# Loading every wide operand of a two-part sequence kernel by transposing transfers, and reordering all of its operations

## The chip, the cores and the metric

The kernel runs on one core of a Trainium2 chip. A core has five engines with an instruction stream each: TensorE (PE, matrix products; its weight loads are listed as PEld), VectorE (DVE), ScalarE (ACT), GpSimd (POOL) and SyncE (SP). SP computes nothing here: it issues the transfers (DMAs), in the order of its stream, and so its stream is called the SP queue below. PE writes its results to PSUM, which has eight banks; DVE or ACT must copy them to SBUF (an eviction) before a bank can be used again. The metric is the device time of one execution in microseconds (us).

## The reference

All inputs and the output are bf16. There are two independent heads over S = 2048 steps and D = 640 channels, and their results are concatenated on the channel axis to [1, 2048, 1280].

```python
# head A: a diagonal complex state-space model
dt = exp(log_dt); Lam_bar = exp(dt * (Lambda_re + 1j * Lambda_im))
B_bar = ((Lam_bar - 1) / Lam)[:, None] * (B_re + 1j * B_im)
Bu = einsum("bld,pd->blp", x, B_bar)
for t in range(L):
    h = Lam_bar * h + Bu[:, t, :]                 # 2048 steps, 640 complex states
y = 2 * einsum("blp,dp->bld", hseq, C).real + x * Dskip
# head B: a short and a long convolution over time, channel by channel
k_shift = sum(k_pad[:, t:t + S] * shift_k[:, 3 - t] for t in range(4))
kv = k_shift * v
y = irfft(rfft(kv_pad) * rfft(ssm_k_pad))[:S] + kv * ssm_D
out_B = q * y
```

## The kernel before, in words

One SBUF tile (`arena`) holds all data; regions are named by `LAY`. Every operation is added to a `Program` with its reads and writes, and `emit` issues all operations in the order written out by hand in the string `ORDER`: each token is operation number, engine letter (T PE, V DVE, A ACT, G POOL, S SP) and first PSUM bank. Each engine works through its own tokens in order. `emit` asks for a wait wherever an operation's footprint touches that of an earlier one on another engine or of an earlier transfer; and it declares two operations independent only where neither is already known to come before the other. For pairs that it leaves undeclared, the framework adds waits by its own view of the addresses. Besides, transfers share eight completion counters in turn, so that a transfer waits for the one eight transfers earlier.

**Head A** (class `PartA`). Time is split as 16 rows i by 128 columns; the 640 complex states are 10 blocks j of 64 states, each with real and imaginary parts on 128 partitions. `load_x` (L478) and `load_B` (L472) load x and B in natural layout. `turn_x` (L503, evicted at L508) transposes x on PE; `prep_B` (L522, evicted at L528) transposes B and multiplies it by a complex factor `GM` (made at L420) that comes from the parameters, which are loaded at L340, transposed on PE (L348) and worked on by small DVE and ACT operations of `params`. The product with x is `base` (L533), five 128x512 matmuls for each half PSUM group; `up2`, `up1`, `up0` combine rows i pairwise by rotation matrices `RR` (L552); `coarse` scans over the 128 columns; `down` distributes back (L655; where ACT evicts, an identity matmul at L653 adds the old value on PE). `project` (L687, L692) multiplies by C, evicts at L696 and stores. C goes through a DRAM plane (L488) and one transposing transfer (L489).

**Head B** (class `PartB`), in two halves of 320 channels. k, v, q are loaded in blocks of 80 channels with time on partitions (`load_k` L755 and L759, `load_v` L768). `conv` multiplies and adds the four taps and v on DVE over 128x2560 tiles (L795, L800, L801). `s1` (L820, evicted at L825) and `s2` (L838, evicted at L851) are the two steps of a transform, for the filter ("h") and for kv ("k"); in `s1` for "k" the weights are columns 40 elements apart. `product` (L862 to L869) is the complex product on DVE, four chunks in a half; `r2` (L883, L888) and `r1` (L904, L916 with the factor q) are the inverse.

`setup` makes the transform matrices with iota (POOL), integer operations and Sin on ACT. L286 and L289 make the arguments of `W`; L325 scales `G`.

Of the kernel before, what the change touches and what calls it, by code (L numbers as in the profile page):

```python
# [182 lines left out]
for _name, _n in (("A", 10 * 16 * 130), ("BT", 6400), ("RR", 5120), ("W", 4096), ("G", 8192), ("XT", 10240), ("AS", 10240),  # L183
                  ("Y", 10240), ("T", 7680), ("H0", 5120), ("K0", 5504), ("V0", 5120), ("YS", 2560), ("SN", 1024), ("I3", 192), ("E", 64),
                  ("JS", 128), ("F1", 128), ("IDF", 192), ("DG", 640), ("SK", 640), ("DM", 160),
                  ("PV", 70), ("SMALL", 1400)):
    LAY.part(_name, _n)


class Ctx:  # L190
    def __init__(self, nc, tc, arena, psum, ins, out):
# [3 lines left out]
        self.CP = {nc.scalar: nc.scalar.copy, nc.vector: nc.vector.tensor_copy, nc.gpsimd: nc.gpsimd.tensor_copy}  # L195
        self.small_at = LAY.at["SMALL"][0]
# [19 lines left out]
def setup(c):  # L216
# [13 lines left out]
    P.add("js0", {V: .2}, lambda e: e.tensor_scalar_mul(out=JS[:, 0:64], in0=I3[:, 64:128], scalar1=-1.0), outs=[JS[:, 0:64]],  # L230
          ins=[I3[:, 64:128]])
    P.add("js1", {V: .2}, lambda e: e.tensor_copy(out=JS[:, 64:128], in_=I3[:, 128:192]), outs=[JS[:, 64:128]],
# [24 lines left out]
    scr = c.arena[:, LAY.at["A"][0]:LAY.at["A"][0] + 20800]  # L257
    m1 = scr[:, 20000:20064].bitcast(i32)
    q1 = scr[:, 20064:20192].bitcast(i32)
    s1 = scr[:, 20192:20320].bitcast(f32)  # L260
# [12 lines left out]
    offw = f(2)  # L273
    for lo, b, val in ((0, 0, 6144.0), (0, 1, 8192.0), (64, 0, 4096.0), (64, 1, 6144.0)):
        P.add("offw", {V: .1}, lambda e, lo=lo, b=b, val=val: e.memset(offw[lo:lo + 64, b:b + 1], val),
              outs=[offw[lo:lo + 64, b:b + 1]])
    mw = scr[:, 0:4096].bitcast(i32)
    qw = scr[:, 4096:12288].bitcast(i32)
    for ch in range(4):
        mc = mw[:, 512 * ch:512 * ch + 512]  # L280
        qc = qw[:, 1024 * ch:1024 * ch + 1024]
        q4 = qc.rearrange("p (k b c) -> p k b c", k=8, b=2)
        P.add("w_m", {G: .6}, lambda e, mc=mc, ch=ch: e.iota(mc, pattern=[[4, 8], [128, 64]], base=1 + 32 * ch,
                                                               channel_multiplier=0), outs=[mc])
        for b in range(2):
            P.add("w_q", {A: .8}, lambda e, q4=q4, mc=mc, b=b: e.activation(  # L286
                out=q4[:, :, b, :], in_=mc.rearrange("p (k c) -> p k c", k=8), func=FN.Identity, scale=p63, bias=offw[:, b:b + 1]),
                outs=[q4[:, :, b, :]], ins=[mc, p63, offw])
        P.add("w_a", {V: .7}, lambda e, qc=qc: e.tensor_single_scalar(out=qc, in_=qc, scalar=8191, op=ALU.bitwise_and),  # L289
              outs=[qc], ins=[qc])  # L290
        wo = Wt[:, 8 * ch:8 * ch + 8, :].rearrange("p k c -> p (k c)")
        P.add("w_s", {A: 1.15}, lambda e, qc=qc, wo=wo: e.activation(out=wo, in_=qc, func=FN.Sin, bias=npi, scale=SC13),
              outs=[wo], ins=[qc, npi])

    IDF = c.IDF = v("IDF")
    mi = scr[:, 20320:20448].bitcast(i32)
    qi = scr[:, 19000:19384].bitcast(i32)
# [14 lines left out]
    sn = v("SN")  # L312
    for ch in range(4):
# [9 lines left out]
        for el in range(2):  # L323
            go = Gt[:, ri, 32 * bh:32 * bh + 32, el, :]
            P.add("g_k", {V: .47, G: 2.9}, lambda e, go=go, el=el: e.tensor_scalar(  # L325
                out=go, in0=sn.rearrange("p (b a) -> p b a", a=32), scalar1=mk[:, el:el + 1], scalar2=None, op0=ALU.mult),
                outs=[go], ins=[sn, mk])


def params(c):  # L330
# [42 lines left out]
    for lo, mi, val in ((0, 0, 2 ** 30), (0, 1, -2 ** 31), (64, 0, 0), (64, 1, 2 ** 30)):  # L373
# [18 lines left out]
    dc, sg = f(2), f(1)  # L392
    for lo, mi, val in ((0, 0, 1.0), (0, 1, 0.0), (64, 0, 0.0), (64, 1, 1.0)):
        P.add("dc", {V: .1}, lambda e, lo=lo, mi=mi, val=val: e.memset(dc[lo:lo + 64, mi:mi + 1], val), outs=[dc[lo:lo + 64, mi:mi + 1]])
    for lo, val in ((0, 2.0), (64, -2.0)):
        P.add("sg", {V: .1}, lambda e, lo=lo, val=val: e.memset(sg[lo:lo + 64, :], val), outs=[sg[lo:lo + 64, :]])
    na, ma, mb, ga = f(20), f(20), f(20), f(20)
# [7 lines left out]
    P.add("den", {V: .12}, lambda e: e.tensor_scalar(out=den, in0=den, scalar1=sg, scalar2=None, op0=ALU.mult), outs=[den], ins=[den, sg])  # L405
    P.add("na", {V: .13}, lambda e: e.tensor_tensor(out=t3(na), in0=al3[:, 0:10, :], in1=bc(dc.rearrange("p (o m) -> p o m", o=1), [128, 10, 2]),
                                                    op=ALU.subtract), outs=[na], ins=[al3[:, 0:10, :], dc])
    P.add("ma", {V: .13}, lambda e: e.tensor_tensor(out=t3(ma), in0=t3(na), in1=bc(col(lre), [128, 10, 2]), op=ALU.mult), outs=[ma], ins=[na, lre])
    P.add("mb", {V: .13}, lambda e: e.tensor_tensor(out=t3(mb), in0=t3(na), in1=bc(col(lim), [128, 10, 2]), op=ALU.mult), outs=[mb], ins=[na, lim])
    P.add("ga0", {V: .12}, lambda e: e.tensor_tensor(out=t3(ga)[:, :, 0], in0=t3(ma)[:, :, 0], in1=t3(mb)[:, :, 1], op=ALU.subtract),  # L410
          outs=[t3(ga)[:, :, 0]], ins=[t3(ma)[:, :, 0], t3(mb)[:, :, 1]])
    P.add("ga1", {V: .12}, lambda e: e.tensor_tensor(out=t3(ga)[:, :, 1], in0=t3(mb)[:, :, 0], in1=t3(ma)[:, :, 1], op=ALU.add),
          outs=[t3(ga)[:, :, 1]], ins=[t3(mb)[:, :, 0], t3(ma)[:, :, 1]])
    P.add("ga", {V: .13}, lambda e: e.tensor_tensor(out=t3(ga), in0=t3(ga), in1=bc(col(den), [128, 10, 2]), op=ALU.mult), outs=[ga], ins=[ga, den])
    scr = c.arena[:, LAY.at["A"][0]:LAY.at["A"][0] + 20800]
    c.GM = scr[:, 17600:18880]
# [6 lines left out]
    spread("gm", c.GM, ga, {V: 1.55})  # L423
# [7 lines left out]
    s16 = v("K0", 5120, 256).bitcast(i32)  # L431
    phs, phc = v("K0", 0, 2560).bitcast(i32), v("K0", 2560, 2560).bitcast(i32)
# [20 lines left out]
class PartA:  # L453
# [57 lines left out]
    def prep_B(self, u):  # L511
# [15 lines left out]
        def ev(e, B):  # L527
            c.CP[e](out=out, in_=B[:, 0:n])  # L528
# [611 lines left out]
```

## Time and profile before

| | |
|---|---|
| median of 3 runs | 229.06 us (228.41 to 230.14) |
| profiled execution: own time | 229.08 us |
| profiled execution: span, first to last instruction | 227.3 us |
| mean granted TensorE clock | 0.959 |
| busy: PE, DVE, ACT, POOL | 197.0, 181.6, 145.0, 47.4 us |
| moved by the transfers | 24.06 MB, 106 GB/s in the mean |

The profiled execution takes 1.8 us more than its span and is as long as the median run. Busy is time in which an instruction of the engine is under way; matmuls overlap, so the busy time of a group over its count is the time that one costs, and the mean ns of one is its latency. A row gives source line, engine, operation, output and inputs; brackets give the idle time before it and what ended it. SPq and ACTq rows are the issuing of transfers. In the timelines, rows of one kind are merged, with their count.

### The profile page before, as it was taken

To read this page: it belongs to the slowest core of one execution; us is meant where nothing else is said; L and a number is where in the kernel's file an instruction comes from. 1 tells how busy PE (TensorE), PEld (TensorE's weight loads), DVE (VectorE), ACT (ScalarE), POOL (GpSimd) and SP (SyncE) were. 2 spreads that over 40 slices of the span, in tenths; PEclk is the share of its full clock that TensorE was granted. 3 is DMA by queue.
4 is the path that set the end of the run, shared out by engine and by line. 5 is a ranking of instruction groups with operands and counts; after the bars stand their busy time and mean duration, and the time that the engine had idled before them with its cause. 6 is when DMAs were issued, how large, how long until landed. Compare 5 with 4: busy or idle time off the path is not lost.

```text
span 227.3 us, 7898 instructions
## 1 busy us (share of the span) xinstructions
PE 197.0 (87%) x3552; PEld 142.6 (63%) x3566; DVE 181.6 (80%) x217; ACT 145.0 (64%) x173; POOL 47.4 (21%) x45
## 2 busy tenths in 40 slices
PE   0715998999999999999999689997999899997793
PEld 0615544545565687786763566776888787777572
DVE  6797698969999956479999999997962489988730
ACT  2870868849669665579889779757764585148021
POOL 6592091000009400500006900074000000000000
PEclk9975899999999999999999999999979699999998
DMA  5999639999900996394992019031503700016264
GB/s 168 243 219 185 157 63 144 121 151 165 172 1 6 115 138 99 57 217 85 150 143 58 4 33 199 12 89 39 112 32 86 179 3 29 31 38 167 59 147 120
DMA packets 96782, 24.06 MB, mean 106 GB/s; under 512 B 91117, under 2 KB 96749, under 8 KB 96749
## 3 DMA queue, kind: packets, MB, share of 16 engines
q1 hardware_dynamic: 96678, 23.56, 58.7%
q8 instruction: 28, 0.46, 0.9%
q14 instruction: 6, 0.04, 0.1%
q10 hardware_dynamic: 70, 0.01, 0.0%
HBM read 16.68 MB, written 6.88 MB: 104 GB/s over the span
## 4 chain that ended last, share of the span: by engine, by line
PE 61%; DVE 25%; ACT 7%; issue 4%; DMA 1%; ACTq 0%; DVEq 0%
PE acc L687 20%; PE acc L820 10%; PE acc L838 7%; PE acc L533 7%; DVE arena L795 6%; PE acc L883 4%; DVE arena L800 4%; PE acc L692 2%; PE acc L904 2%; PE acc L503 2%; PE acc L522 2%; PE acc L552 1%; PE acc L655 1%; DVE arena L801 1%; DVE arena L420 1%
## 5 line engine op out<-in xcount | busy, mean ns | idle before, releaser
L687 PE MATMUL acc<-arena 128*128 128x320 bf16 x320 | 49.9, 306 | 0.0
L533 PE MATMUL acc<-arena 128*128 128x512 bf16 x188 | 43.9, 381 | 1.7 <-issue 1.3
L825 ACT CAST arena<-acc 128x1024 bf16<-128x1024 f32 x34 | 33.7, 1015 | 11.0 <-PE acc L820 10.9
L687 PEld LDWEIGHTS <-arena 128*128 128x128 bf16 x320 | 29.9, 100 | 12.7 <-issue 1.6
L851 ACT CAST arena<-acc 128x960 bf16<-128x960 f32 (+1 forms) x39 | 34.6, 919 | 4.9 <-PE acc L838 4.3
L696 ACT CAST arena<-acc 128x640 bf16<-128x640 f32 x16 | 11.0, 692 | 33.1 <-PE acc L692 33.1
L533 PEld LDWEIGHTS <-arena 128*128 128x128 bf16 x200 | 18.7, 99 | 20.5 <-issue 0.8
L820 PE MATMUL acc<-arena 64*64 64x64 bf16 x1280 | 28.8, 238 | 1.5 <-DVE arena L673 0.8
L820 PEld LDWEIGHTS <-arena 64*64 64x64 bf16 x1280 | 26.3, 159 | 5.9 <-issue 2.1
L838 PE MATMUL acc<-arena 128*64 128x160 bf16 x512 | 22.5, 244 | 2.1 <-ACT arena L825 1.1
L795 DVE TENSOR_TENSOR arena<-arena 128x2560 bf16<-128x2560 bf16 x15 | 23.7, 1593 | 0.3
L838 PEld LDWEIGHTS <-arena 128*64 128x64 bf16 x512 | 19.2, 115 | 5.0 <-ACT arena L825 1.6
L800 DVE TENSOR_TENSOR arena<-arena 128x2560 bf16<-128x2560 bf16 x12 | 18.8, 1568 | 0.3
L916 DVE TENSOR_TENSOR arena<-acc,arena 128x960 bf16<-128x960 f32 (+1 forms) x12 | 12.1, 1041 | 5.1 <-PE acc L904 5.0
L888 ACT CAST arena<-acc 128x1024 bf16<-128x1024 f32 x13 | 13.1, 1021 | 2.1 <-PE acc L883 1.7
L883 PE MATMUL acc<-arena 64*128 64x128 bf16 x320 | 12.1, 226 | 2.6 <-DVE arena L869 1.7
L671 ACT CAST arena<-acc 128x1024 bf16<-128x1024 f32 (+2 forms) x16 | 13.9, 933 | 0.2 <-PE acc L655 0.2
L825 DVE CAST arena<-acc 128x1024 bf16<-128x1024 f32 x6 | 7.3, 1219 | 8.3 <-ACT arena L825 6.2
L655 PE MATMUL acc<-arena 128*128 128x512 bf16 (+2 forms) x50 | 13.8, 326 | 0.0
L883 PEld LDWEIGHTS <-arena 64*128 64x128 bf16 x320 | 11.0, 145 | 4.5 <-ACT arena L671 2.2
L865 DVE TENSOR_TENSOR arena<-arena 128x1280 bf16<-128x1280 bf16 x16 | 12.8, 822 | 0.8
L862 DVE TENSOR_TENSOR arena<-arena 128x2560 bf16<-128x2560 bf16 x8 | 11.9, 1492 | 1.2 <-ACT arena L851 0.5
(134 smaller groups left out, 287.9 us busy)
## 6 DMA issues: line engine op xcount, KB each, us to landing
out_dram<-arena SPq DMA_DIRECT2D x32, 160.0 KB
arena<-in_A_x_dram SPq DMA_DIRECT2D x16, 160.0 KB
arena<-in_B_ssm_k_dram SPq DMA_DIRECT2D x8, 320.0 KB
arena<-in_B_k_dram SPq DMA_DIRECT2D x8, 320.0 KB
arena<-in_B_v_dram SPq DMA_DIRECT2D x8, 320.0 KB
arena<-in_B_q_dram SPq DMA_DIRECT2D x8, 320.0 KB
arena<-in_A_B_re_dram SPq DMA_DIRECT2D x2, 400.0 KB
arena<-in_A_B_im_dram SPq DMA_DIRECT2D x2, 400.0 KB
```

What stands on the lines that cost most here:

```text
L533: e.matmul(o, lhsT=self.BT[:, j, d, :], rhs=self.XT[:, d, t0:t0 + n], start=(d == 0), stop=(d == 4), skip_group_check=True)
L655: e.matmul(B[:, o:o + 128 * k], lhsT=c.RR[:, n, j, :], rhs=A[:, j, q:q + k, 0:128], start=not by_pe, stop=True, skip_group_check=True)
L671: e.copy(out=o, in_=b)
L687: e.matmul(B[:, 512 * b:512 * b + 320], lhsT=lh[j], rhs=self.CT[:, j, 320 * b:320 * b + 320], start=(j == 0), stop=False, skip_group_check ...
L795: P.add(f"cv{hf}m", cost, lambda e: e.tensor_tensor(out=out, in0=k, in1=bc(s, [128, 64, 40]), op=ALU.mult), outs=[out], ins=[k, c.SK[:, hf ...
L800: P.add(f"cv{hf}a", cost, lambda e, t1=t1: e.tensor_tensor(out=t1, in0=t1, in1=T2, op=ALU.add), outs=[t1], ins=[t1, T2])
L820: e.matmul(B[64 * b:64 * b + 64, 512 * l + 64 * i:512 * l + 64 * i + 64], lhsT=lh[i][ps], rhs=F[ps, b, :], start=True, stop=True, tile_pos ...
L825: P.add(f"e1{what}{hf}_{u}", {PACT: act(1024), PDVE: dve(1024)}, lambda e, B: c.CP[e](out=out, in_=B.rearrange("p (l n k s) -> p k s l n", ...
L838: e.matmul(B[64 * s:64 * s + 64, 512 * b + 160 * i:512 * b + 160 * i + 160], lhsT=c.W[:, k, 64 * b:64 * b + 64], rhs=self.AS[:, k, 160 * s ...
L851: c.CP[e](out=out, in_=b.rearrange("p r (k j n) -> p r k j n", k=n, j=4) if nj > 1 else b.rearrange("p r (k x) -> p r k x", k=n))
L883: e.matmul(B[:, 512 * s + 128 * i:512 * s + 128 * i + 128], lhsT=lh[i][s][r], rhs=rh, start=(r == 0), stop=(r == 1), tile_position=(64 * s ...
L888: P.add(f"er2{hf}_{u}", {PACT: act(1024), PDVE: dve(1024)}, lambda e, B: c.CP[e](out=out, in_=B.rearrange("p (s n b) -> p b s n", s=2, n=4 ...
```

## The change

- **Loads.** B, x, C, k and v are loaded by transposing transfers straight from the inputs: 20 for B (64 by 640 elements each), 16 for x (128 by 640), 2 for C (640 by 640), 5 each for k and v (2048 by 128). `turn_x`, `prep_B` and the DRAM plane of C go.
- **Factor.** The factor of B is applied to C instead: `scale_C` (40 matmuls of 128x320 on 64 rows each, 10 evictions of 128x640).
- **Short convolution.** Channels lie on partitions, five blocks d of 128 channels by 2048 steps. A tap is a product with a per-partition scalar, on DVE or ACT (`cm{d}_{j}`); additions `ca{d}_{j}` and the product with v `cx{d}` on DVE or POOL. The result goes to DRAM (`plane`) and comes back with time on partitions (`relay`), so that `s1` for "k" now reads weights that are contiguous. There is one buffer for k and three for v.
- **Setup.** The arguments of `W` are one integer product on POOL (`w_q`, four of them) in place of eight ACT and four DVE operations; scaling of `G` may run on ACT.
- **Order.** `up2` takes two blocks j and one quarter of time; `ORDER` is new throughout. In the changed kernel's string 141 is the copy of the taps' weights (`sw`), 373, 374, 376, 378 are `cm0_3` to `cm0_0`, 77 is the Exp of dt, 80 to 84 are Exps, 22 (`f1_s`), 135, 136, 102 and 47 (`i_s`) are Sins, 163 to 178 load x (x0 to x15), 143 to 162 load B, 371, 382, 393 load k, 372, 383, 394 load v, 204 to 222 (even) are `up2`.

```diff
     def load_B(self, a):
         for ri, src in ((0, c.ins["A_B_re"]), (1, c.ins["A_B_im"])):
+            dst = self.BT[:, a, :, 64 * ri:64 * ri + 64]
+            s = src[64 * a:64 * a + 64, :].rearrange("p (d q) -> p d q", q=128)
+            P.add(f"ld_B{a}", {PSP: .36}, lambda e, dst=dst, s=s: e.dma_start_transpose(out=dst, in_=s), outs=[dst], nbytes=64 * 1280)
     def load_x(self, i):
-        dst = self.xn[:, i, :]
-        s = self.x2.rearrange("(s r) d -> r s d", r=16)[ROW0[i]]
-        P.add(f"ld_x{i}", {PSP: .45}, lambda e: e.dma_start(out=dst, in_=s), outs=[dst], nbytes=128 * 1280)
+        dst = self.XT[:, :, 128 * i:128 * i + 128]
+        s = self.x2.rearrange("(s r) (d q) -> r s d q", r=16, q=128)[ROW0[i]]
+        P.add(f"ld_x{i}", {PSP: .72}, lambda e: e.dma_start_transpose(out=dst, in_=s), outs=[dst], nbytes=128 * 1280)
...
-    def turn_x(self, u):
-    def prep_B(self, u):
+    def scale_C(self, a, h):
+        def mm(e, B):
+            for r in range(2):
+                for j in range(2):
+                    ps = slice(64 * j, 64 * j + 64)
+                    e.matmul(B[:, 512 * j:512 * j + 320], lhsT=gm[ps, r, a, :], rhs=self.CR[ps, r, a, cs], start=(r == 0), stop=(r == 1),
+                             tile_position=(64 * j, 0))
...
-    def up2(self, j):
+    def up2(self, j0, q):
+            for a in range(2):
+                self.base(e, B[:, 512 * a:512 * a + 512], j0 + a, 1024 + 512 * q)
...
+    def load_kv(self, d):
+        for n, out, x in (("k", c.v("KT", 16, 2048), self.k2), ("v", c.v("VT", 2048 * (d % 3), 2048), self.v2)):
+            P.add(f"ld_{n}{d}", {PSP: 2.3}, lambda e, out=out, x=x: e.dma_start_transpose(out=out, in_=x[:, 128 * d:128 * d + 128]),
+                  outs=[out], nbytes=2048 * 256)
...
+    def conv(self, d):
+        at = 16
+        Vt, t1, t2 = c.v("VT", 2048 * (d % 3), 2048), self.T[:, 2560:4608], self.T[:, 4608:6656]
+        tt = {PDVE: dve(2048, .52), PPOOL: 4.5}
+        def tap(out, j):
+            k, w = c.v("KT", at - j, 2048), c.SW[:, 4 * d + j:4 * d + j + 1]
+            P.add(f"cm{d}_{j}", {PDVE: .7, PACT: act(2048)}, lambda e: c.SM[e](out, k, w), outs=[out], ins=[k, w])
+        tap(t1, 3)
+        for j in (2, 1, 0):
+            tap(t2, j)
+            P.add(f"ca{d}_{j}", tt, lambda e: e.tensor_tensor(out=t1, in0=t1, in1=t2, op=ALU.add), outs=[t1], ins=[t1, t2])
+        P.add(f"cx{d}", tt, lambda e: e.tensor_tensor(out=Vt, in0=t1, in1=Vt, op=ALU.mult), outs=[Vt], ins=[t1, Vt])
+    def plane(self, d):
+        P.add(f"pl{d}", {PSP: 1.6}, lambda e: e.dma_start(out=c.kvdram[128 * d:128 * d + 128, :], in_=vt), outs=[tok], ins=[vt],
+              nbytes=128 * 4096)
+    def relay(self, hf):
+        for x in range(4):
+            lo = 320 * hf + 80 * x
+            dst = self.KV[32 * x:32 * x + 32]
+            src = c.kvdram[lo:lo + 80, :].rearrange("n (a b) -> a n b", b=64)
+            P.add(f"rl{hf}_{x}", {PSP: 2.3}, lambda e, dst=dst, src=src: e.dma_start(out=dst, in_=src), outs=[dst],
+                  ins=[c.tok[:, lo // 128:(lo + 79) // 128 + 1]], nbytes=80 * 4096)
...
-            lh = [self.kv[x // 40].rearrange("p (b n) -> p b n", n=40)[:, :, x % 40] for x in gs]
+            lh = [self.KV[:, x, :] for x in gs]
...
 ORDER = (
+    "178S0 142V0 42G0 105V0 70V0 132G0 73A0 6G0 371S0 71A0 1G0 72A0 8V0 74A0 0G0 12V0 137S0 7V0 96G0 2V0 131G0 144S0 9V0 27V0 75T6 "
+    "14V0 18G0 3V0 15G0 146S0 76V6 95G0 109V0 77A0 138G0 177S0 10V0 78V0 55G0 11V0 145S0 19V0 85V0 86V0 44V0 176S0 48V0 16V0 87V0 "
+    "20V0 65G0 107V0 43V0 88V0 24V0 79V0 89V0 143S0 90V0 25V0 108V0 21V0 110V0 175S0 91V0 45V0 46V0 151S0 92V0 133G0 153S0 141A0 "
+    "373A0 173S0 152S0 154S0 171S0 22A0 93G0 94G0 374A0 97G0 172S0 98G0 134G0 174S0 147S0 214T6 162S0 135A0 375V0 150S0 148S0 33G0 "
+    "82A0 83A0 156S0 136A0 218T2 149S0 111V0 215V6 80A0 376A0 158S0 99G0 100G0 169S0 101G0 17V0 50G0 161S0 23V0 104V0 204T0 26V0 "
+    "139S0 102A0 155S0 377V0 81A0 47A0 219A2 170S0 159S0 103V0 160S0 378A0 106V0 112V0 49V0 208T4 113V0 51G0 372S0 114V0 157S0 "
+    "168S0 382S0 56G0 167S0 206T2 52A0 205V0 165S0 383S0 209A4 379V0 53A0 30G0 222T0 180S0 182S0 207A2 116V0 115V0 164S0 126V0 60G0 "
...
```

More of the change, by code (lines that the diff above doesn't have):

```diff
@@ L495, in turn_x @@
         g = P.group(2)
[L496 to L497 removed]
+        gm = c.GM.rearrange("p (r a m) -> p r a m", r=2, a=5)
+        cs = slice(320 * h, 320 * h + 320)
         def mm(e, B):
[L500 to L504 removed]
```

266 lines of the change are left out of this document (100 added, 166 removed), and 63 rows, old and new, of the table ORDER.

## The prediction

> **What bounds the kernel now.** I read the page's busy times and slices first, then three stretches, then the timelines.
>
> ```profile
> PE 197.0 (87%) x3552; PEld 142.6 (63%) x3566; DVE 181.6 (80%) x217; ACT 145.0 (64%) x173; POOL 47.4 (21%) x45
> ...
> PE   0715998999999999999999689997999899997793
> ```
>
> PE is full from the fourth slice (5.7 us each) on: it sets the end, and its empty start is the one large gap. The stretches are cut at the start of the first `up0a` (57.8) and of the first `r2` (126.4); columns: length, then busy us of PE, PEld, DVE, ACT, POOL.
>
> ```profile
> 0.00:57.80 57.80, 41.61 (x570) 25.72 (x578) 48.36 (x89) 37.55 (x46) 20.17 (x36) 0.91 0.93 161
> 57.80:126.40 68.60, 65.67 (x883) 44.67 (x890) 58.46 (x62) 51.33 (x64) 16.14 (x8) 1.00 0.69 101
> 126.40:223.60 97.20, 89.76 (x2100) 72.25 (x2100) 74.83 (x68) 55.49 (x64) 11.14 (x2) 0.96 0.35 78
> ```
>
> In the middle stretch PE is idle for 3 of 68.6 us, but DVE has only 10 us to spare: whatever adds to DVE there becomes visible. The timeline gives the unit prices on PE, and shows what kept it waiting at the start and at the middle.
>
> ```profile
> 19.75 3.57 PE L522 MATMUL acc<-arena 128*128 128x128 bf16 x32 [6.96 <-DVE arena L420]
> ...
> 26.78 2.32 PE L533 MATMUL acc<-arena 128*128 128x512 bf16 x10
> ```
> ```profile
> 56.91 0.71 PE L820 MATMUL acc<-arena 64*64 64x64 bf16 x64
> ...
> 126.41 0.72 PE L883 MATMUL acc<-arena 64*128 64x128 bf16 x16 [1.74 <-DVE arena L869]
> ```
> ```profile
> 163.63 4.01 PE L820 MATMUL acc<-arena 64*64 64x64 bf16 x128
> ```
>
> At the start PE waits for the factor `GM` (L420), the end of a chain of small operations. An `s1` group of 32 matmuls takes 0.36 us with contiguous weights ("h", 64 in 0.71) and 1.0 with strided ones ("k", 128 in 4.01; other rows give 1.15): I take 1.08 and 0.37.
>
> **PE, part by part.** Gone: `turn_x` 7.0 us (L503), `prep_B` 4.9 (L522), both busy times; twenty "k" groups at 0.71 less, 14.2; identity matmuls, since ACT now does 7 of the 21 `down` evictions in place of 16: 12 of 128x512 at 0.216 and 9 of 128x256 at 0.11, 3.6. Added: 40 matmuls of `scale_C`, not in the trace; below, half of a full-row 128x320 (`project`, 0.136 each) as two row halves run together, 2.7 us; above 5.4; I take 4.5. PE: 197.0 - 29.7 + 4.5 = 172. If PE alone set the end, that would be some 25 us saved.
>
> **What it costs elsewhere.** (1) *ACT's function tables.* In the new order ACT runs, one after another: Exp (dt), tap, Sin, tap, Sin, two Exps, Sin, Exp, tap, Sin, Exp, Sin (`i_s`), and later one Exp between Sins. The built program has ten table loads for two before, seven between dt and the first eviction on ACT.
>
> ```profile
> 7.88 0.80 ACT L286 ACTIVATE arena<-arena 128x512 int32<-128x512 int32 x1
> 8.69 1.28 ACT L386 ACT_TABLE_LOAD   x1
> 9.99 0.27 ACT L386 ACTIVATE arena<-arena 128x80 f32<-128x80 int32 x1
> ```
>
> The operation before ends at 8.68 and the next begins at 9.99: 1.30 a load, 9.1 for seven. (The Trainium skill, "ScalarE: Activation LUTs", section "What ACT_TABLE_LOAD costs", puts a drain of some 1.38 us on top of 1.28; this row shows none. By the page the seven would cost 18.6.)
>
> (2) *The chain of x.* In the built order of the changed kernel each x transfer waits, beyond the counter that it shares, for the landing of the x transfer before it: their strided destinations interleave in address, so the framework orders them, and all of SP's queue stands behind. The price of a hop comes from the one transposing transfer in the trace, 50 blocks of 128x128 (1.64 MB); columns of the second view: stretch, busy us as above, clock, DMA share, GB/s.
>
> ```profile
> 93.47 7.61 SPq L489 DMA_TRANSPOSE arena<-c_planes  x1
> ```
> ```profile
> 101.00:102.00 1.00, 0.86 (x25) 0.80 (x26) 0.92 (x1) 1.00 (x2) 0.00 (x0) 1.00 1.27 290
> 102.00:103.00 1.00, 0.84 (x23) 0.62 (x20) 0.81 (x1) 1.00 (x3) 0.00 (x0) 1.00 0.86 195
> 103.00:104.00 1.00, 1.00 (x30) 0.82 (x28) 1.00 (x2) 1.00 (x2) 0.00 (x0) 1.00 0.00 0
> ```
>
> Issuing takes 0.152 us a block: 0.76 for an x (5 blocks), 0.38 for a B, 2.43 for a k or v, 3.8 for a C. Issuing ends at 101.08 and data at 102.7, so I add 1.8 to landing: a hop is 2.6. No row shows so small a transposing transfer; the bounds are 2.1 (the tiny parameter load, issued at 2.08, used at 4.22) and 4 (twice the wait for landing).
>
> **The start, added up.** SP: x15 0.7, k0 1.5 to 3.9, four B's, x14 5.0, x13 7.6, x12 10.2, lands 12.8; there the first `up2` begins, 7 us before today's first large product. Then x10 12.8, x8 15.4, x9 18.0, x11 20.6 (second quarter 23), seven B's, x6 24, x7 28.6, v0 30.1 to 32.5, x5 33, k1 33.7 to 36.1, x4 36.1 (lands 38.7: `up1` can start), and x3, which `up0a` needs, 52, lands 54.6.
> ACT: dt 5.1 as now; eight taps by 2048 at 1.87 (0.16 + 0.00083 an element, from 1.02 for 1024) 15.0; loads 9.1; eight evictions 8.1; three Sins and four scalings of `G` 7.3; four Sins of `W` 4.6; sin, cos and small ones 5; waits for k0 1 and, at `cm1_2`, for k1 (32.5 to 37.9) 5.4. Sum 60.6: then the last Sin of `W` is done, which every `s1` eviction needs (its target is the scratch of `W`). The last `up1` eviction, which frees the bank of `up0a`, is at 59.6.
> PE: ten `up2` 21.9 and five `up1` 13.1 with their waits are done by 57. So `up0a` starts near **60**, against 57.8 today, but with all 15 groups of `up2` and `up1` behind it, where today there are 12.
>
> **The middle.** From 60.8 on DVE has in its order, up to the last product: four complex products of 1.49 + 2 x 0.82 + 0.92 + 0.82, 19.5; eight taps; seven additions and products with v of 128x2048 at 1.22 (scaled from 1.49 for 2560), 8.5; eleven `s1`, `s2`, `up0`, `scale_C` and nine `down` evictions, 21.4; both scans with their products 10.1; three spreads at 1.48, 4.4; small ones 1.5. A tap on DVE is a tensor by a per-partition scalar, as L325:
>
> ```profile
> L325 DVE TENSOR_SCALAR arena<-arena x6: 473/480/1903, 50.9 to 144.8; 128x1024 bf16<-128x1024 bf16 x6
> ```
>
> 0.48 for 1024 gives 0.80 for 2048; above, the rate of two-input operations, 1.22 (if k read at an odd element loses the fast form); I take 0.80, 6.4. Sum 71.8. The maximum of 1.90 in that row is at 129.58, while POOL works until 131.2; POOL has 22 us to do in the same stretch (`r16`, `dg`, two `ca4`, `cx4`), so I add 3, and 2 for waits. The first `r2` comes at 60.8 + 76.8 = **137.6**, 11 later than today. PE's own work in between, 65.6, and ACT's, 66, would be done by 127: DVE is the bound, and PE's saving in this stretch is covered.
>
> **The rest.** Today 86.3 us of PE work (by the unit prices) take 100.9, that is 14.6 of waits, slower clock and tail. After: 69.2, of which 8.5 less for "k" groups. There the bound changes by the phase: `s2` and `s1` of the second half are limited by ACT (12.5), the four products by DVE (23.9). The larger of the engines, phase by phase: 15.3 + 12.5 + 23.9 + 8.4 + 11.7 = 71.8; with the same 14.6, **86.4**.
> Span 137.6 + 86.4 = 224; outside it 1.8, minus rounding: **225** against the profiled 229.08 (and the same median). A difference of 1% is about what a measurement of this kernel can tell from none.
>
> **Rivals.**
> *Faster, short hops (about 214).* If small transfers land 2.1 after issue, 14 hops give 7 back, and if POOL does not hold DVE up another 3 to 4. For it: the queue has slack while ACT loads tables; PE's total is 25 lower. Chance 0.2.
> *Slower, long hops (about 236).* A hop of 3.4 moves x4 and k1 from 36 to 47 (14 x 0.8); ACT stands at `cm1_2`, and `up0a` and DVE's stretch shift with it: 225 + 11. It is slower by over 1% from a hop of 3.05 on. For it: B's and k's share the rings with x, and data stalled for over a microsecond within the trace's transposing transfer (104 and 46 GB/s in 98 to 100 us, between 305 and 290). Against: that transfer's end lay only 1.6 behind its issue. Chance 0.29.
> *Slower, a drain with each table load (about 234).* If a switch waits for the pipeline between back-to-back operations, seven times 1.38 come on top of ACT's chain, which leads to 60.6. The row above shows no such wait, but it is one row. This is the page's rule. Chance 0.04.
> *The new layout does not speed "k" up (about 231).* The groups keep 1.08: PE has 13 us of slack in the middle but none in the rest, where 7 come back. Against it: "h" groups with contiguous weights cost 0.36 in every row. Chance 0.05.
> *My forecast, 225 (218 to 231).* Chance 0.42.
>
> **How the numbers follow.** Faster by over 1% (below 226.8): 0.2 plus somewhat over half of the forecast's 0.42, with the low tail of the others, 0.47. Within 1%: 0.17. Slower: 0.36. The range takes in the hop's bounds (225 - 11 to 225 + 14) and the taps' 1.22 (8 x 0.42 = 3.4, inside): 214 to 239. The forecast's own range crosses the present time, so the sign is weakly held.
>
> **What would show it.** Right: ten ACT_TABLE_LOAD rows; x transfers on SP one landing apart, about 2.6 us; first `up2` near 13, first `up0a` near 60, DVE over 90% busy from there to the first `r2` near 138; "k" groups at 0.37; PE busy near 172. Wrong, if x transfers issue back to back, if a tap on DVE takes over 1.3, if `r2` starts before 128 or the rest takes over 95.

## The result, and the profile after

The changed kernel takes **255.15 us** (median of 4, 254.25 to 256.77) where the kernel before takes 229.60 in the same comparison: 1.112 times as long (95% interval 1.102 to 1.121). The prediction was 225 (214 to 239), so it named the wrong side, and the time lies outside its range. The profiled execution takes 254.25 us; its span is 252.4, against 227.3 before. (Some executions of these programs run 1.5% and more longer at a lower clock; the ratios leave them out, so that a range can reach further than a ratio suggests, and the profiles of e5_start and e9_spread are of such executions.)

The page of the changed kernel, busy times and PE's 40 slices (6.3 us each):

```profile
PE 185.9 (74%) x3445; PEld 121.0 (48%) x3455; DVE 162.4 (64%) x218; ACT 155.3 (62%) x179; POOL 46.5 (18%) x46
...
PE   0046472589962899797679999867686999997890
```

PE's sum did fall, from 197.0 to 185.9, and the span grew all the same. The slices say where: where PE was full from the fourth slice on, it now stands at 2 to 7 tenths up to the thirteenth, but for a short run of 8 and 9. The three stretches, cut at the same two events as before (the first `up0a`, whose first weights load at 82.7, and the first `r2`, 158.5); columns: length, busy us of PE, PEld, DVE, ACT, POOL, then clock, share of the transfer engines, GB/s:

```profile
0.00:82.70 82.70, 43.46 (x254) 18.17 (x257) 35.02 (x82) 50.52 (x50) 31.09 (x40) 0.89 0.62 113
82.70:158.50 75.80, 67.16 (x1171) 43.34 (x1179) 67.11 (x79) 58.41 (x78) 15.44 (x6) 0.97 0.61 126
158.50:252.40 93.90, 75.25 (x2020) 59.47 (x2020) 60.23 (x59) 46.41 (x52) 0.00 (x0) 0.94 0.42 90
```

| stretch | before | predicted | measured | measured less predicted |
|---|---|---|---|---|
| to the first `up0a` | 57.8 | 60 | 82.7 | +22.7 |
| `up0a` to the first `r2` | 68.6 | 77.6 | 75.8 | -1.8 |
| first `r2` to the end | 100.9 | 86.4 | 93.9 | +7.5 |
| span | 227.3 | 224 | 252.4 | +28.4 |

In the first stretch no engine is full: PE is busy for half of it, DVE for less, ACT for 61%. PE and ACT wait for loads, DVE for PE and ACT, and the loads for the SP queue. The rows for the lines that load x (L482) and B (L476); columns: issue time in ns, minimum, median and maximum, then the first and the last start in us:

```profile
L482 SPq DMA_TRANSPOSE arena<-in_A_x_dram x16: 1199/1217/2694, 0.7 to 77.4; - x16
...
L476 SPq DMA_TRANSPOSE arena<-in_A_B_im_dram x10: 1197/1254/1256, 4.9 to 44.4; - x10
```

A transfer of B keeps SP for 1.25 us where I had priced 0.38, and one of x for 1.22 where I had 0.76. The timeline of the SP queue shows it nearly without pauses (68.3 of the 77.4 us ahead of the last row are issuing, and 5.2 are waits for x to land); a row with x2 is two issues:

```profile
8.80 1.25 SPq L476 DMA_TRANSPOSE arena<-in_A_B_re_dram  x1
10.28 1.21 SPq L482 DMA_TRANSPOSE arena<-in_A_x_dram  x1
11.53 1.25 SPq L476 DMA_TRANSPOSE arena<-in_A_B_re_dram  x1
13.23 1.20 SPq L482 DMA_TRANSPOSE arena<-in_A_x_dram  x1
14.48 2.55 SPq L476 DMA_TRANSPOSE arena<-in_A_B_re_dram  x2
...
50.51 2.63 SPq L725 DMA_TRANSPOSE arena<-in_B_k_dram  x1
...
63.31 2.46 SPq L482 DMA_TRANSPOSE arena<-in_A_x_dram  x1
...
70.77 2.69 SPq L482 DMA_TRANSPOSE arena<-in_A_x_dram  x1
...
77.42 1.23 SPq L482 DMA_TRANSPOSE arena<-in_A_x_dram  x1
```

The second block of k comes at 50.5 in place of 33.7, and x3, the row that `up0a` waits for, is issued at 77.4 in place of 52. Two of the last issues of x take twice the usual time (2.46 and 2.69). ACT's timeline shows what that does to the taps, and one of the ten table loads:

```profile
7.60 2.00 ACT L197 ACTIVATE arena<-arena 128x2048 bf16<-128x2048 bf16 x1
9.62 1.28 ACT L269 ACT_TABLE_LOAD   x1
10.91 0.35 ACT L269 ACTIVATE arena<-arena 128x64 f32<-128x64 int32 x1
...
55.71 2.00 ACT L197 ACTIVATE arena<-arena 128x2048 bf16<-128x2048 bf16 x1 [15.34 <-DMA arena<-in_B_k_dram]
```

ACT stands for 15.3 us before a tap, until k's second block lands. PE's timeline, and one row of 5 us stretches of the same kernel (its eighth column is the granted clock):

```profile
47.04 8.13 PE L512 MATMUL acc<-arena 128*128 128x512 bf16 x30 [7.72 <-DMA arena<-in_A_B_im_dram]
...
97.07 0.71 PE L788 MATMUL acc<-arena 64*64 64x64 bf16 x64
```
```profile
45.00:50.00 5.00, 2.96 (x8) 1.03 (x9) 0.00 (x0) 0.00 (x0) 0.00 (x0) 0.50 0.63 139
```

PE, too, waits for B (7.7 us). After this wait it runs for 3 us at a granted clock of 0.50: eight wide products begin in those 2.96 us, where at 0.216 it would be thirteen. The second PE row is as predicted: 64 products of `s1` for "k" (L788) in 0.71, 0.36 a group.

In the last stretch PE stands idle between small products with no releaser that the profile shows ("issue"):

```profile
167.42 0.88 PE L788 MATMUL acc<-arena 64*64 64x64 bf16 x45
170.02 0.48 PE L788 MATMUL acc<-arena 64*64 64x64 bf16 x19 [1.72 <-issue]
...
172.29 1.08 PE L788 MATMUL acc<-arena 64*64 64x64 bf16 x77
174.30 0.35 PE L788 MATMUL acc<-arena 64*64 64x64 bf16 x19 [0.93 <-issue]
...
175.76 0.47 PE L872 MATMUL acc<-arena 64*64 64x80 bf16 x29 [0.43 <-ACT arena L793]
178.58 0.66 PE L872 MATMUL acc<-arena 64*64 64x80 bf16 x51 [2.34 <-issue]
```

The breaks lie in the middle of groups (45 and 19 are 64 products of one pair of groups). Adding up the counts of all rows between, these three lie exactly 128 products apart. There are five such breaks behind the first `r2`, 8.2 us in all; the kernel before has two, 1.9 us.

### The profile page after: what moved, and what is told of

The parts are those of the page before. It is cut to its first block, busy times and chain, and to the rows that moved or that the text cites. A ratio compares the mean times of both kernels' runs of the same rounds, so it can differ in the third digit from the quotient of the medians.

```text
span 252.4 us, 7739 instructions
## 1 busy us (share of the span) xinstructions
PE 185.9 (74%) x3445; PEld 121.0 (48%) x3455; DVE 162.4 (64%) x218; ACT 155.3 (62%) x179; POOL 46.5 (18%) x46
## 4 chain that ended last, share of the span: by engine, by line
PE 32%; DVE 24%; SPq 14%; DMA 12%; issue 9%; ACT 6%; DVEq 0%; ACTq 0%
PE acc L512 12%; DMA arena<-in_A_x_dram 8%; SPq L476 7%; PE acc L666 6%; DVE arena L830 5%; DVE arena L833 5%; DVE arena L652 4%; PE acc L851 4%; SPq L482 3%; PE acc L788 3%; DVE arena L819 3%; DVE arena L835 2%; PE acc L531 2%; PE acc L872 2%; DMA arena<-kv_rows 2%
## 5 line engine op out<-in xcount | busy, mean ns | idle before, releaser
L512 PE MATMUL acc<-arena 128*128 128x512 bf16 x193 | 52.9, 430 | 29.8 <-DMA arena<-in_A_x_dram 16.9
L666 PE MATMUL acc<-arena 128*128 128x320 bf16 x320 | 49.8, 305 | 0.0
L512 PEld LDWEIGHTS <-arena 128*128 128x128 bf16 x200 | 20.6, 107 | 59.0 <-issue 36.5
L197 ACT ACTIVATE arena<-arena 128x2048 bf16<-128x2048 bf16 (+3 forms) x20 | 26.7, 1346 | 21.0 <-DMA arena<-in_B_k_dram 19.3
L819 ACT CAST arena<-acc 128x960 bf16<-128x960 f32 (+1 forms) x34 | 30.3, 916 | 10.2 <-PE acc L806 9.7
L793 ACT CAST arena<-acc 128x1024 bf16<-128x1024 f32 x31 | 30.0, 1025 | 7.9 <-PE acc L788 7.6
L788 PE MATMUL acc<-arena 64*64 64x64 bf16 x1280 | 17.7, 201 | 11.8 <-issue 4.9
L751 DVE TENSOR_TENSOR arena<-arena 128x2048 bf16<-128x2048 bf16 x13 | 16.7, 1284 | 14.0 <-ACT arena L197 13.9
L788 PEld LDWEIGHTS <-arena 64*64 64x64 bf16 x1280 | 14.0, 113 | 17.3 <-issue 7.3
L528 DVE CAST arena<-acc 128x1024 bf16<-128x1024 f32 x4 | 5.0, 1256 | 22.5 <-PE acc L512 22.5
L652 DVE TENSOR_TENSOR arena<-acc,arena 128x1024 bf16<-128x1024 f32 (+2 forms) x14 | 15.4, 1133 | 1.3 <-PE acc L634 1.2
L287 POOL TENSOR_TENSOR arena<-arena 128x1024 int32<-128x1024 int32 x4 | 9.1, 2292 | 28.8 <-DVE arena L281 28.7
L856 ACT CAST arena<-acc 128x1024 bf16<-128x1024 f32 x12 | 11.9, 1017 | 3.2 <-PE acc L851 3.0
```

The lines of the kernel that those rows point to most:

```text
L197: self.SM = {nc.scalar: lambda out, in_, by: nc.scalar.mul(out, in_, by), nc.vector: vm(nc.vector), nc.gpsimd: vm(nc.gpsimd)}
L512: e.matmul(o, lhsT=self.BT[:, j, d, :], rhs=self.XT[:, d, t0:t0 + n], start=(d == 0), stop=(d == 4), skip_group_check=True)
L652: e.tensor_tensor(out=o, in0=b, in1=o, op=ALU.add)
L666: e.matmul(B[:, 512 * b:512 * b + 320], lhsT=lh[j], rhs=self.CT[:, j, 320 * b:320 * b + 320], start=(j == 0), stop=False, skip_group_check ...
L751: P.add(f"ca{d}_{j}", tt, lambda e: e.tensor_tensor(out=t1, in0=t1, in1=t2, op=ALU.add), outs=[t1], ins=[t1, t2])
L788: e.matmul(B[64 * b:64 * b + 64, 512 * l + 64 * i:512 * l + 64 * i + 64], lhsT=lh[i][ps], rhs=F[ps, b, :], start=True, stop=True, tile_pos ...
```

## The experiments

Theories for the start: (T1) the price of issuing a small transposing transfer; (R1) the chain of landings of x, which the prediction has as a main cost; (R2) ACT's table loads, which it has on the path. For the end: PE's instruction stream, against PE's own time and the engines behind it.

**e1_price: the price of an issue, on a chip that does nothing else.** The program is replaced by transfers, each of which waits for the one before.

```diff
+        P.add("t64x1", tr, lambda e: e.dma_start_transpose(out=t(1, 64), in_=dd(Bre[0:64, 0:128])), ...)
+        P.add("t64x5", tr, lambda e: e.dma_start_transpose(out=t(5, 64), in_=dd(Bre[0:64, :])), ...)
+        P.add("t128x1", ...)
+        P.add("t128x5", ...)
+        P.add("t128x5 rows 16 apart", ...)
+        P.add("t320x5", ...)
+        P.add("t640x5", ...)
...
+        P.add("plain 128x640", tr, lambda e: e.dma_start(out=t(5, 128), in_=xs[3]), ...)
```

> Leaves out all computation: the kernel only issues transfers on SP and stores zeros. Each of eleven transfers (10 transposing, 1 plain, in two passes) waits for the landing of the one before it; then 8 of B's kind, 8 of x's kind and 4 of k's kind are issued back to back. Theory (issue price): in the changed kernel each transposing transfer of x and of B kept SP for 1.20 to 1.25 us, with 128 rows and with 64 alike; it is the price of issuing itself. Then an idle chip shows the same: 1.2 to 1.3 us for five blocks, at 64 rows and at 128, about 2.1 for k (16 blocks), 3.6 for five blocks of 640 rows. Rival (full rings): the issue is held up by transfers that are still under way; then it is 0.4 for 64 rows and 0.75 for 128 on an idle chip, and grows only in the runs back to back.

Timeline of its SP queue; L915 to L921 are the first seven lines of the diff in order, L925 is the last, L928 is the run of eight of B's kind:

```profile
0.73 1.18 SPq L915 DMA_TRANSPOSE arena<-in_A_B_re_dram  x1
3.01 1.21 SPq L916 DMA_TRANSPOSE arena<-in_A_B_re_dram  x1
5.50 1.12 SPq L917 DMA_TRANSPOSE arena<-in_A_B_im_dram  x1
...
13.54 1.41 SPq L920 DMA_TRANSPOSE arena<-in_A_B_im_dram  x1
17.50 3.09 SPq L921 DMA_TRANSPOSE arena<-in_A_B_re_dram  x1
...
35.79 0.37 SPq L925 DMA_DIRECT2D arena<-in_A_x_dram  x1
...
75.68 10.26 SPq L928 DMA_TRANSPOSE arena<-in_A_B_im_dram  x8
```

One block of 64 rows costs 1.18 to issue (1.12 with 128 rows), five blocks of 64 rows 1.21, five of 128 rows 1.22 (with rows 16 apart 1.21), five of 320 rows 1.41, five of 640 rows 3.09, 16 blocks of k 2.08; the plain transfer of the same x 0.37. So there is a floor of about 1.1 us under each transposing transfer of the sizes tried, and the time per block begins to count only above it. Back to back it is 1.28. T1 holds for these sizes: it is the issue, not full rings. It does not cover every issue: the two of x above took 2.46 and 2.69, and 24 of k's kind back to back took 1.3 to 4.2 each (e7 below) where one alone takes 2.1 to 2.3. What holds these longer ones was not tried.

**e2_b_plane: B alone, by a DRAM plane.**

```diff
-    20 transposing transfers of 64x640 (load_B)
+            P.add("bp", ..., lambda e, ...: e.dma_start(out=dst, in_=s), ...)               # re, im -> b_rows [1280, 640]
+        for lo, hi in ((0, 768), (768, 1280)):
+            P.add("ld_B", ..., lambda e, ...: e.dma_start_transpose(out=dst, in_=s), ...)   # from b_rows
```

> B alone: the 20 transposing transfers become two plain copies into one DRAM plane and two transposing transfers from it. Theory (issue price): 25.0 us of issuing on SP become about 8.6 (two of 0.6, two of some 3.7); the first product with the last rows of x (up0a), which came at 82.7 us, comes at 66 to 70, since the chain of landings of x is then partly bare; the span falls from 252.4 by 10 to 16, to 236 to 243. Rival (the chain of landings of x sets the start): up0a stays at 80 to 83 and the span within 2 us of 252. Rival (ACT's table loads set the start): the same, no change.

Measured: 252.14 us (250.18 to 253.10), ratio 1.098 (1.089 to 1.107); `up0a` at 77.5, first `r2` at 152.9, span 251.3. A miss for T1's numbers: 5.2 us came at `up0a`, not 13 to 17. Two things in the trace fit the rest: SP now waits 12.9 us for x (5.2 in the changed kernel), so the chain lies bare; and the plane is not cheap, the issue of k0 behind its copies takes 6.5 us in place of 2.2.

**e3_x_rows: the layout of x alone.**

```diff
-        self.XT = v("XT").rearrange("p (d t) -> p d t", d=5)
+        self.XT = v("XT").rearrange("p (i d s) -> p i d s", i=16, d=5)
-        dst = self.XT[:, :, 128 * i:128 * i + 128]
+        dst = self.XT[:, i]
```

> The layout of x in SBUF becomes row by row (row, block, column), so that the destinations of the 16 transfers of x no longer interleave and none waits for the landing of the one before; the matrix products read the same data in pieces of 128 columns. Theory (issue price): only the 5.2 us that SP waited for x go; up0a at 77 to 82, span 247 to 252. Rival (chain of landings): 13 hops of 2.8 become issues of 1.25, up0a at 62 or earlier and the span near 232.

Measured: 248.90 us (248.27 to 249.91), ratio 1.087 (1.080 to 1.094); `up0a` at 76.2, first `r2` at 149.6, span 247.5. T1's numbers but for 0.8 us at `up0a`; R1's 62 and 232 are excluded. The chain of landings was there (its hop measures 2.8 us, I had 2.6), but the 20 issues of B lay in its gaps.

**e4_tables: the five Exps ahead of the first Sin.**

```diff
-  ... 373A0 (tap) 22A0 (Sin) 374A0 135A0 (Sin) 82A0 83A0 (Exp) 136A0 (Sin) 80A0 (Exp) 376A0 102A0 (Sin) 81A0 (Exp) ... 84A0 (Exp)
+  ... 373A0 (tap) 80A0 81A0 82A0 83A0 84A0 (Exp) 22A0 (Sin) 374A0 135A0 136A0 376A0 102A0 ...
```

> The five Exps of the powers (operations 80 to 84) are moved in front of the first Sin, so that ACT loads its function tables twice or three times in place of ten. Theory (SP's queue sets the start): the 10 us of table loads that go turn into waiting for k; span 250 to 253. Rival (ACT's chain sets the start): 8 to 10 us less, span 242 to 245.

Measured: 255.59 us (252.62 to 258.87), ratio 1.111 (1.100 to 1.122), the same as the changed kernel; `up0a` at 81.5. The table loads go, and ACT, done earlier, waits for PE's products with late loads (7.1 and 5.8 us) and still 14.7 us for k. R2 as the one cause is excluded. In the rows of the changed kernel shown above, the tap before the table load ends at 9.60, the load begins at 9.62 and the next operation 0.01 behind its end: there is no drain, against the Trainium skill, "ScalarE: Activation LUTs", section "What ACT_TABLE_LOAD costs", which puts one of some 1.38 us on each load.

**e5_start: all repairs of the start, B by the plane.** The diffs of e2 to e4 together, the plain copies issued by ACT, the small load of D ahead of x.

> All repairs of the start at once: B through one DRAM plane (its two plain copies issued by ACT) and two transposing transfers, the row-by-row layout of x, the five Exps ahead of the first Sin, the small load of D ahead of x. Theory (SP's issuing, the chain of x and ACT's tables each cover the next): none gave much alone, together they do; SP's issuing ahead of x3 adds up to some 55 us with its waits, up0a at 58 to 66 (82.7 before the repairs), the first r2 at 136 to 145 (158.5), the rest 94 to 98 as measured before, so a span of 232 to 242. Rival (the transfers themselves, at 150 to 250 GB/s, hold the start): up0a at 72 or later and a span of 244 or more. Rival (the rest is bound as the prediction has it, 86): span 224 to 230.

Measured: 241.15 us (236.54 to 241.68); `up0a` at 69.5, first `r2` at 141.9, span 239.1. Between the theories at `up0a`. Its SP queue names the reason:

```profile
2.11 12.27 SPq L728 DMA_TRANSPOSE arena<-in_B_k_dram  x1
```

The issue of k0 took 12.3 us behind the two copies from DRAM to DRAM, and the parameters, whose first product was at 6.6, came at 19.0; the start was shifted as a whole.

**e8_start2: the same without the plane.** B comes by two transposing transfers of 640x640 into free columns, and four copies on DVE bring it into place.

```diff
+        for ri, src in ((0, c.ins["A_B_re"]), (1, c.ins["A_B_im"])):
+            dst, s = c.v("Y", 3200 * ri, 3200).rearrange("p (d x) -> p d x", d=5), src.rearrange("x (d q) -> x d q", q=128)
+            P.add("ld_B", {PSP: 3.1}, lambda e, dst=dst, s=s: e.dma_start_transpose(out=dst, in_=s), ...)
+                P.add("cp_B", {PDVE: 1.0}, lambda e, out=out, x=x: c.CP[e](out=out, in_=x), ...)
```

> As the run with all repairs of the start, but B without the DRAM plane: two transposing transfers of 640x640 into free columns (Y), and four copies on DVE that put real and imaginary parts side by side. In the run with the plane the two plain copies held the transfer rings, so that the load of k0 took 12.3 us to issue, the parameters came 10 us later and x14 was issued at 23.3. Theory (SP's issuing): x14 at 14 to 15, up0a at 59 to 64 (69.5 with the plane), the first r2 at 131 to 137 (141.9), the rest still 94 to 98, span 227 to 234. Rival (other transfers in the stretch to 60 hold x back as before): up0a at 67 or later, span 237 or more.

Measured: **227.50 us** (227.27 to 231.05), ratio to the kernel before 0.987 (0.975 to 0.9995). Its stretches, cut at the same events (columns as above):

```profile
0.00:60.30 60.30, 38.72 (x258) 17.17 (x259) 39.35 (x84) 40.56 (x43) 35.23 (x40) 1.00 0.80 158
60.30:131.60 71.30, 65.43 (x1175) 42.53 (x1179) 69.06 (x81) 57.63 (x77) 15.95 (x6) 1.00 0.63 128
131.60:225.10 93.50, 74.69 (x2020) 59.87 (x2020) 60.18 (x59) 46.41 (x52) 0.00 (x0) 0.94 0.43 93
```

`up0a` is at 60.3, 22.4 earlier than in the changed kernel, which is all but 0.3 of its miss in the first stretch; the middle stretch is 4.5 shorter, with DVE busy for 69.1 of 71.3 us; the last is as long as it was. It has the lowest time of this study, 1.3% below the kernel before, but the interval all but reaches 1: that it is faster is not shown.

**e11_b_y: B alone, in the way of e8.**

> B alone, without the DRAM plane: two transposing transfers of 640x640 and four copies on DVE in place of 20 transposing transfers; the chain of landings of x and ACT's ten table loads stay as they are. Theory (SP's issuing and the chain of x cover each other): 25.0 us of issuing become about 6.9, but then the chain (a hop of 2.8 us) is bare: up0a at 69 to 74 (82.7 in the changed kernel, 60.3 with all repairs, 76.2 with the layout of x alone), span 238 to 246. Rival (the issuing of B alone makes the whole loss): up0a at 65 or earlier and a span near 230. Rival (the chain of x alone): up0a at 80 or later, span 250 or more.

Measured: 248.01 us (244.31 to 249.64), ratio 1.073 (1.063 to 1.082); `up0a` at 73.8, first `r2` at 147.7, span 242.5. Inside the first theory for both (the profiled execution is the shortest of the four); both rivals are excluded. What ends the last wait ahead of `up0a` here is no load any more, but ACT, whose L292 is the Sin of `W`:

```profile
73.85 4.03 PE L517 MATMUL acc<-arena 128*128 128x512 bf16 x10 [2.85 <-ACT arena L292]
```

So `up0a` gains 8.9 by B alone, 6.5 by x alone, 1.2 by the tables alone (one profile each), and 22.4 by all three: more than the sum of 16.6, since each hid behind the others. (e8 also moves the small load of D, which stood in the chain of x; this was not tried by itself.)

**e6_fetch and e7_fetch_busy: 2048 products of `s1` and nothing else,** first on an idle chip, then beside 24 transposing transfers.

```diff
+    for u in range(64):
+        P.add(f"s1_{u}", {PPE: .4}, mm, ins=[w, f], group=P.group(2), nmm=32)
+    for i in range(24):                                                     # e7 only
+        P.add("busy", {PSP: 2.1}, lambda e, d=d, i=i: e.dma_start_transpose(out=d, in_=k2[...]), ...)
```

> Leaves out everything but 2048 matrix products of 64x64 in the pattern of s1, in a row on PE without any wait, while no transfer runs; the output is zeros. Theory (PE's stream is fetched in blocks of 256 instructions, 128 products with their weight loads): after the first blocks there are idle times exactly 128 products apart, and a block takes 3 to 4 us where the products need 1.5; 2048 products take 40 to 60 us. Rival (only busy transfers hold the stream up): 0.0117 us each, 24 us in all, no idle time.

> The same 2048 products while SP issues 24 transposing transfers of k's kind (2048 rows by 128). Both theories: longer than without transfers. Blocks that are fetched through the same transfer engines: 4 to 5.5 us a block, as in the stretch from 160 to 190 us of the changed kernel (5.4, 3.5, 5.4, 3.7, 4.0 in the run with x row by row), 55 to 80 us in all. If it takes as long as the idle case, transfers do not matter.

PE's timeline of e6, then of e7:

```profile
1.24 3.06 PE L915 MATMUL acc<-arena 64*64 64x64 bf16 x223 [1.24 <-DVE arena L906]
6.28 1.24 PE L915 MATMUL acc<-arena 64*64 64x64 bf16 x128 [1.98 <-issue]
...
34.58 1.92 PE L915 MATMUL acc<-arena 64*64 64x64 bf16 x128 [1.53 <-issue]
38.03 1.92 PE L915 MATMUL acc<-arena 64*64 64x64 bf16 x128 [1.53 <-issue]
```
```profile
42.80 1.92 PE L915 MATMUL acc<-arena 64*64 64x64 bf16 x128 [3.72 <-issue]
48.17 1.92 PE L915 MATMUL acc<-arena 64*64 64x64 bf16 x128 [3.45 <-issue]
```

The first 223 products run through; then PE stops after every 128, without any wait in the program. A block takes 3.45 to 3.73 us on the idle chip (4.3 to 4.8 in the first 20 us, where the stores of the output ran) and 4.0 to 5.7 beside transfers; the products need 1.24 at full clock. From 20 us on the granted clock is 0.50 in e6, so that of the least block, 3.45, 1.92 are products at the half clock and 1.53 are the stop. PE's whole row ends at 60 and at 78 us, where 2048 products at 0.0117 would be 24. The theory holds on both counts. The Trainium skill, "Runtime: NRT & Kernel Launch", section "Instruction fetch mechanics", says that each engine's stream is refilled in blocks of 256 instructions and that the cost of a boundary is mostly hidden. The block agrees (128 products with 128 weight loads); hidden it is not here, for products this small.

The transfers confirm that the stops are the stream's. The pages count packets, MB and the share of the transfer engines by queue; e6, then the changed kernel:

```profile
q8 instruction: 15, 0.25, 1.6%
```
```profile
q8 instruction: 27, 0.44, 0.7%
```

These are packets of 16 KB. In the traces of e6 and e7 each of the 15 stops has one of them, and PE goes on 1.2 to 1.6 us after it has landed; for the five stops of the changed kernel behind the first `r2` it is 1.2 to 1.7 us. The kernel before fetches as much (28 packets) and has 1.9 us of such stops; that its slower small products cover the rest is an argument, not a measurement.

**e9_spread: wide products between the small ones.** Four groups of `project` are moved forward.

```diff
-  ... s1 r1 s2 s1 (small)  C7 C11 C8 C6 C5 C12 C10  r2  C9 r1 C14 r1 C13 C15
+  ... s1 C7 s1 C11 r1 C8 s2 s1 C6 s1 (small)  C5 C12 C10 C9 C14 C13 C15  r2  r1
```

> The changed kernel with one thing altered: four of the last eleven groups of project (26 wide products in 3.2 us each) stand four places earlier, between the groups of s1, r1 and s2 where PE stood idle without a visible reason (8 us in all after the first r2); the last seven follow in the old places, PSUM banks are given out anew. Theory (PE's stream comes in blocks of 128 small products at 3.5 to 5.5 us, the wide products need few instructions and cover the fetching): 6 to 11 us less, span 241 to 246, idle time of that kind below 4 us. Rival (the idle time has another cause, or the stretch is bound by DVE and ACT): the work only changes place, span 249 to 254.

Measured: 257.17 us (254.62 to 259.04), ratio 1.108 (1.094 to 1.122): a miss, and the rival's case: the ratio is that of the changed kernel (1.112). The phases behind the first `r2`, from PE's timelines (the last column is the sum of PE's idle times there that no releaser ends):

| | first `r2` to last `r1` of half 0 | to the last `s1` | to `r2` of half 1 | to PE's end | tail | sum | "issue" |
|---|---|---|---|---|---|---|---|
| before | 29.8 | 21.1 | 25.6 | 20.6 | 3.8 | 100.9 | 1.9 |
| changed | 25.2 | 11.3 | 26.9 | 24.3 | 6.2 | 93.9 | 8.2 |
| e9_spread | 34.3 | 14.8 | 27.1 | 12.9 | 11.2 | 100.3 | 5.5 |
| e12_half_s1 | 24.2 | 10.6 | 29.0 | 21.2 | 5.8 | 90.8 | 5.0 |

The idle time of this kind does fall, from 8.2 to 5.5 (expected: below 4). But the first two phases grow by 12.6, the whole length of the four groups (4 x 3.2): a group of `project` is longer than the idle time that it stands in, and (this is read from the order and not tried) what waits behind it on PE feeds ACT and DVE, on which the next phases depend.

**e10_both: e8 and e9 together.**

> Both of the two before: repairs of the start without the plane, and four groups of project moved between small products. Theory: the gains add, since one lies before the first up0a and the other behind the first r2: 227 to 234 less 6 to 11, span 217 to 227, faster than the kernel before (its span is 227.3). Rival (what is saved at the start is given back behind the first r2): 229 to 236.

Measured: 231.84 us (229.48 to 234.59), ratio 1.004 (0.999 to 1.010), span 229.7: 4.3 us slower than e8 in the median. The rival's case, for e9's reason: against e8, the first two phases grow from 25.6 and 11.8 to 34.1 and 14.4, though the idle time falls from 9.2 to 3.4.

**e12_half_s1: 320 small products left out** in the second half of head B.

```diff
-            for i in range(8):
+            for i in range(0, 8, 1 + hf):
```

> The changed kernel without every second product of s1 in the second half of head B (h and k, 320 of 640 products with their weight loads); evictions and all else stay. These products take 0.0117 us each on PE, 3.7 us. Theory (behind the first r2 PE waits for its stream, 128 products a block, 3.5 to 5.4 us a block): 2.5 blocks fewer, so 7 to 11 us less behind the first r2 (93.9 in the changed kernel, so 83 to 87) and about half as much unexplained idle time there (8 us). Rival (PE's own time): at most 3.7 less, 90 to 94. Rival (evictions and DVE bind there): 0 to 2 less.

Measured: 248.73 us (246.18 to 249.95), ratio 1.078 (1.071 to 1.086); behind the first `r2` 90.8, 3.1 less than the changed kernel. The theory's 83 to 87 is missed, and the number lies where the rival "PE's own time" has it. The idle time without a releaser falls by as much (8.2 to 5.0, last column of the table above), so the two can't be told apart here. Nor is 3.1 a precise size: in the seven profiles that have the same 2020 products behind the first `r2` (the changed kernel, e2 to e5, e8, e11), they take 93.5 to 98.9, with 8.2 to 13.4 of such idle time. What is shown is that the stream stops PE; that its 8 us are the reason for the 7.5 which the prediction lacks behind the first `r2` is not shown.

## Why the prediction was wrong, step by step

- **PE's sum: 172, measured 185.9.** The parts that were priced from rows are right: `scale_C` 4.0 (taken 4.5), `project` 49.8 (49.9 before), "k" groups 0.36 (0.37). The products with x (L512) took 52.9 in place of 43.9, 9 us for the same work: from 22.1 to 26.1, 29.4 to 33.0, 47.0 to 50.0 and 83.0 to 87.0 us, all behind idle times, the granted clock was 0.50 to 0.59. `s1` took 17.7 in place of 14.6. The Trainium skill, "TensorE: Matmul & The Clock Gate", section "Part 1: The HAM clock gate (the "warmup" mystery)", has the array at half rate after an idle window of some 3.4 us until it has been busy as long; the row of 45 to 50 us, behind 7.7 us of waiting, agrees, but this alone does not give the 0.59 from 22.1 us on, behind an idle time of 2.05. The prediction had no term for the clock; it is a consequence of the late loads more than a cause: in e8 the products with x take 47.4, and PE's sum is 178.8.
- **(1) ACT's function tables.** Ten loads, 1.28 each, as predicted, and no drain (that rival had 0.04). But the 9.1 us were put on a chain "which leads to 60.6", and e4 shows them to be covered as long as the loads come late; with B repaired, ACT is the last to end (e11).
- **(2) The chain of x: the failed step.** "Issuing takes 0.152 us a block: 0.76 for an x (5 blocks), 0.38 for a B" is a rate from one transfer of 50 blocks, used as the price of small ones. Measured: 1.22 and 1.25, with a floor of 1.1 under any size measured (e1). Up to x4 this accounts for the delay: x4 is issued 17.2 late (53.3 for 36.1), where 20 transfers of B at 0.87 more and 11 of x at 0.46 more are 22.5, some of which lay in x's hops. From x4 to x3 the queue takes 24.2 for 15.9. There single issues are longer than the floor (x 2.46 and 2.69, two plain loads of `ssm_k` 1.68 and 1.80), and why is open. Together x3 is issued 25.4 late; the sum had more slack between x3's landing and `up0a`, which came 22.7 late. The bounds were put on the hop's landing (2.1 to 4) and none on the issue, so the range missed too. The hop itself was right: 2.8 for 2.6. The rival "long hops", whose 236 came nearest, had the right place and the wrong mechanism: the three hops in which nothing else was issued take 2.75, 2.82 and 3.07, not 3.4.
- **The start, added up.** With the prices of SP repaired (e8) `up0a` comes at 60.3, where the sum had 60. That sum still had ACT's table loads and x's hops in it, which e8 removes, and the hit is in part luck: x4 is issued at 33.5 (36.1 in the sum), but x3 at 55.5 (52), since the longer issues between them are there in e8 too.
- **The middle: the bound was right.** 75.8 for 77.6, with DVE busy for 67.1 of 75.8 us, a little under the 90% named. Once the loads come in time, as the prediction assumed, it is 69.1 of 71.3 (e8): near the sum of DVE's work, 71.8, without the 5 us added for POOL and waits. A tap on DVE takes 0.75 (taken 0.80), an addition over 2048 columns 1.23 (taken 1.22).
- **The rest: 93.9 for 86.4.** The "k" groups gave what was predicted where `s1` stands: that phase went from 21.1 to 11.3. But the phase from the first `r2` to the last `r1` takes 25.2, where the larger engine had 15.3; of that, 7.0 is PE idle, 5.0 of it in the stream. The other mis-sized phases are the products with their fillers (26.9 for 23.9) and the end (24.3 and a tail of 6.2, for 20.1, with 14.6 of waits in all). How much of the 7.5 each has stays open.
- **Slips in the sums.** 224 and 1.8 are 225.8, not 225. A hop of 4, the upper bound, is 14 x 1.4 = 19.6 more, which puts the range's end at 245, not 239. Ahead of x14 stand two transfers of B, not four. None of this brings 255 into the range. None of the signs that it named as "wrong" came either: none of them was about the issue of a single transfer.
- **The chances.** 0.36 for slower was too low: the step that a row did not show was given one price, where its neighbours among the rows (0.35 to 0.7 us for the issue of plain transfers, 7.61 for 50 transposed blocks) left anything between open.

## What to carry to other kernels

A rate taken from one large transfer is no price for small ones: count the issues on each queue and price them by a row of their own size, or measure one; here 36 issues with a floor of 1.1 us outweighed the 25 us of matrix work that were to be saved (PE's sum fell by 11.1). Where several chains end near the same time, removing one shows less than its share (8.9, 6.5 and 1.2 alone, 22.4 together), so a repair that "does nothing" is not yet refuted. And when small products become faster, look at how fast PE gets its instructions before counting the gain.

## What the runs showed of the hardware

- Issuing a transposing transfer keeps the SP queue for 1.1 to 1.2 us from one block of 64x128 up to five of 128x128, 1.4 for five of 320 rows, 3.1 to 3.4 for five of 640, 2.1 to 2.3 for 16 blocks in a column, 4.0 to 4.2 for 32; a plain one of 128x640 takes 0.33 to 0.37 (e1, one at a time).
- 24 transposing transfers of 0.52 MB back to back moved 12.6 MB in 70.9 us, 177 GB/s; the stores after them ran at about 390 (e7).
- PE stopped after each 128 small products: 3.45 us a block at the least, up to 5.7 beside transfers; the first 223 products run without a stop (e6, e7). Each stop has one packet of 16 KB on the queue of instructions, and ends 1.2 to 1.7 us after its landing.
- Two plain copies of 0.8 MB from DRAM to DRAM, issued first, made the next transposing issue take 6.5 us (issued by SP) or 12.3 us (issued by ACT) in place of 2.2.
- A DVE scan of 128x640 took 3.00 us in the changed kernel beside a POOL addition of 128x2048, 1.49 without; e2, e3 and e11 show the same.
